# A fourth pair tile and a 512-token block with quarter products, in a retention layer followed by a gated feed-forward

## The chip, the cores and the metric

One core of a Trainium2 chip runs the kernel. The metric is the device time in microseconds. Three runs of the kernel before took 306.05, 307.16 and 307.43 us, so the median is 307.16.

## The reference

```python
# q, k, v: 8 batches x 8 heads x 576 positions x 64, float32
scores = scale * np.matmul(q, k.transpose(0, 1, 3, 2))
Dmat = np.where(rel >= 0, gamma[:, None, None] ** rel[None, :, :], 0.0)
attn_out = np.matmul(scores * Dmat[None, :, :, :], v)
x = attn_out.transpose(0, 2, 1, 3).reshape(4608, 512)
gate = 1.0 / (1.0 + np.exp(-(x @ w_gate)))    # 512 x 1536
val = x @ w_val                               # 512 x 1536
out = gate * val @ w_out                      # 1536 x 512
```

The decay by position is folded into two tables, by which q and k are multiplied when they are cast to bf16. What is left of the mask is a triangle of ones.

## The kernel before

The instructions stand in an order that the code writes out; no scheduler moves them. Engines are PE (TensorE), ACT (ScalarE), DVE (VectorE), POOL (GpSimd) and SP, which issues nearly all DMAs. Each engine works through its own queue in order and waits on semaphores.

**Attention.** A batch has 576 positions: four chunks of 128 and a last one of 64, which is put together with that of another batch. Attention within a chunk, or half a chunk, is a masked score product; what lies ahead comes in through a running state per head (k transposed times v). Two forms of this work exist.

- A *pair tile* takes 256 positions of one batch at once (`load_pair`, `cast_pair`, `pair_t`, `pair_qk`, `pair_st`, `third_intra`, `third_inter`, `pair_out`). Its q and k are transposed by PE. Before, there are three: batch 0 and batch 1, positions 0 to 255, and batch 0, positions 256 to 511.
- A *single chunk* or step takes 128 positions (`load_part`, `cast_qk`, `cast_v`, `cross` or `turn_step`, `scores`, `products`, `mask`, `intra`, `inter`). The transposed q and k (T) come by a DMA transpose on SP's queue (`cross`), or from PE for the steps in TURNED (0, 1 and 7). There are 30 steps before. Their matmuls are 64 wide and run in bursts: `slot_of_two` gives in one burst the values of up to two steps and the scores of up to two later ones. EARLY sets the bursts of the first blocks: the number of the place in the block, the steps whose values come, the steps whose scores come.

**Feed-forward.** Tokens go in blocks: 0 to 511, then 512 to 767, 768 to 1023, and from 1024 on blocks of 512. The first three blocks use plain matmuls, 256 columns wide in the blocks 512 and 768 (`h_units`, L817), then output products of 512 columns (`op_units`, L1157). Blocks from 1024 on use quarter products: of each unit of four 128-wide columns of w_gate or w_val, seven products of quarter size with sums of weights and of x take the place of eight. `quarter(kind, u, i)` is one of these, four matmuls of 256 columns (L941); g05 is gate unit 0, product 5, and w14 value unit 1, product 4. A unit has three PSUM banks, called a, g and e and listed in BANKS: the letters f, q, t, p, s are the bank pools. Product 1 goes to a, ACT copies a to g, product 2 is added there; 5 and then 3 go to e; 6, 7 and 4 are added in a. DVE adds what has to be summed, and ACT (gate) or DVE and POOL (value) take the results to SBUF. ORDER is the written order of these products in a block; in it a letter c is a part of a chunk's cast, x1d a sum of x on DVE, o a part of the output product.

The sums of weights are made once: `w_sums` for w_gate and w_val, `wo_sums` for w_out, all on DVE, at places given by SUMS_AT and PLACES in the blocks 512 and 768. The sums of x for a block (`x_sum`) are made on DVE or POOL when its attention is done.

**Queues around the change.** POOL multiplies k and q by the tables and casts v, chunk after chunk. SP issues a chunk's loads, then its transpose behind the loads of the next chunk, so loads stand behind a transpose that waits for POOL. `landing` deals the loads over 18 buffers.

**No-ops.** `space` puts a no-op behind a matmul of PE; SPACES and SPACES_FIRST say how many and in which blocks.

## Time and profile before

| | us |
|---|---|
| median of three runs | 307.16 |
| profiled execution | 306.89 |
| its span, first to last instruction | 305.2 |
| PE busy | 296.5 |
| DVE, ACT, POOL busy | 240.1, 195.0, 208.4 |
| block 512 begins, block 1024 begins (PE) | 53.46, 91.08 |

The span is what lies between the first and the last instruction; the 1.7 us beside it belong to the execution's time but have no instruction. Times in the views count from the span's start. A row of the chain or of a timeline has start, length, engine and what was done; "x8" are eight instructions merged, so that length/8 is the issue time of one.

### The profile page before, as it was taken

How to read it: one execution, taken by the hardware profiler on the slowest of the kernel's cores; microseconds unless marked ns; L12 is line 12 of the kernel's file. 1: busy time of each engine (PE TensorE's matmuls, PEld its weight loads, DVE VectorE, ACT ScalarE, POOL GpSimd, SP SyncE). 2: the span in 40 equal slices, each digit the busy share in tenths (PEclk: the TensorE clock that was granted, in tenths of full speed). 3: DMA queues.
4: the chain of work that ended last, by engine and by line, in shares of the span. 5: the costliest groups of instructions: out<-in, count | busy, mean ns of one | idle time of the engine just before them, and what ended most of it. 6: DMA issues, size and time to landing. Idle time of an engine off the chain costs nothing.

```text
span 305.2 us, 11063 instructions
## 1 busy us (share of the span) xinstructions
PE 296.5 (97%) x4473; PEld 242.7 (80%) x4483; DVE 240.1 (79%) x464; ACT 195.0 (64%) x414; POOL 208.4 (68%) x256
## 2 busy tenths in 40 slices
PE   7899999999999999999999999999999999999994
PEld 6754455876858888888888888888888888888883
DVE  4746786888897899689978997898789968945793
ACT  6534753426539656965796579657965886648640
POOL 5784543746466999769976997699769916741670
PEclk9999999999999999999999999999999999999998
DMA  7999998998999998999599939992960390022004
GB/s 216 317 350 397 358 272 200 211 211 175 188 174 228 188 249 198 237 250 217 134 197 238 198 70 216 231 191 66 229 159 4 102 248 3 2 61 81 2 2 138
DMA packets 145731, 54.99 MB, mean 180 GB/s; under 512 B 124048, under 2 KB 138640, under 8 KB 145680
## 3 DMA queue, kind: packets, MB, share of 16 engines
q1 hardware_dynamic: 144880, 53.63, 74.1%
q8 instruction: 36, 0.59, 0.8%
q10 hardware_dynamic: 800, 0.66, 0.7%
q14 instruction: 15, 0.12, 0.1%
HBM read 37.75 MB, written 9.44 MB: 155 GB/s over the span
## 4 chain that ended last, share of the span: by engine, by line
PE 93%; ACT 2%; DVE 1%; issue 1%; POOL 0%; ACTq 0%; POOLq 0%
PE gatea L941 12%; PE wa L941 12%; PE qa L1055 11%; PE qe L1055 9%; PE gatee L941 6%; PE we L941 6%; PE h_v L817 4%; PE h_g L817 3%; PE op L1157 3%; PE op L1431 3%; PE gateg L941 3%; PE wg L941 3%; PE val L656 2%; PE hv L1281 2%; PE hg L1281 2%; PE row L630 2%
## 5 line engine op out<-in xcount | busy, mean ns | idle before, releaser
L428 POOL TENSOR_TENSOR qk<-k,ktab 128x512 bf16<-128x512 f32 x30 | 32.3, 1078 | 7.0 <-DMA k<-in_k_dram 6.5
L1055 PEld LDWEIGHTS <-gsum 128*128 128x128 bf16 x336 | 31.9, 98 | 4.9 <-DVE gsum L878 0.8
L878 POOL TENSOR_TENSOR gsum<-gv 128x256 bf16<-128x256 bf16 (+1 forms) x35 | 26.8, 774 | 11.6 <-DVE gv L966 10.4
L941 PEld LDWEIGHTS <-wg_sb 128*128 128x128 bf16 x308 | 30.1, 98 | 3.7
L941 PEld LDWEIGHTS <-wv_sb 128*128 128x128 bf16 x308 | 30.1, 98 | 3.5
L428 POOL TENSOR_TENSOR qk<-q,qtab 128x512 bf16<-128x512 f32 x28 | 30.0, 1073 | 4.2 <-DMA q<-in_q_dram 4.2
L941 PEld LDWEIGHTS <-wvt 128*128 128x128 bf16 x280 | 27.4, 98 | 3.3
L941 PEld LDWEIGHTS <-wgt_sb 128*128 128x128 bf16 x252 | 24.6, 98 | 2.9
L1055 PEld LDWEIGHTS <-gv 128*128 128x128 bf16 x240 | 22.9, 98 | 3.1
L878 POOL TENSOR_TENSOR gsum<-gv,gsum 128x256 bf16<-128x256 bf16 x37 | 25.3, 715 | 0.0
L966 POOL TENSOR_TENSOR gv<-gv,wu 128x512 bf16<-128x512 bf16 x7 | 8.1, 1162 | 24.4 <-DVE wu L992 24.4
L645 DVE TENSOR_TENSOR pt<-row,tri 128x256 bf16<-128x256 f32 x60 | 21.2, 412 | 4.4 <-PE row L638 3.9
L433 POOL CAST v<-v 128x512 bf16<-128x512 f32 x20 | 13.7, 686 | 15.1 <-DMA v<-in_v_dram 11.0
L716 ACT CAST xT<-val 128x256 bf16<-128x256 f32 x60 | 18.9, 389 | 6.7 <-PE val L671 6.6
L941 PE MATMUL wa<-xsum,wv_sb 128*128 128x256 bf16 x140 | 21.0, 273 | 0.0
L607 ACT CAST sb<-s 128x256 bf16<-128x256 f32 x46 | 17.8, 418 | 4.6 <-DVE s L743 2.3
L941 PE MATMUL gatea<-xsum,wg_sb 128*128 128x256 bf16 x140 | 19.9, 273 | 0.0
L966 POOL TENSOR_TENSOR gv<-gv,ws 128x512 bf16<-128x512 bf16 x15 | 17.5, 1164 | 2.9 <-DVE ws L995 2.9
L995 DVE TENSOR_TENSOR gs<-gatea,gs 128x512 f32<-128x512 f32 x21 | 13.9, 688 | 6.0 <-PE gatea L941 5.2
L987 DVE TENSOR_TENSOR gatee<-gatea,gs 128x512 f32<-128x512 f32 x14 | 9.8, 699 | 10.2 <-PE gatea L941 7.4
L995 DVE TENSOR_TENSOR ws<-wa,ws 128x512 f32<-128x512 f32 x21 | 14.4, 685 | 4.2 <-PE wa L941 4.1
L964 ACT ACTIVATE gv<-gs 128x512 bf16<-128x512 f32 x21 | 13.0, 630 | 7.0 <-DVE gs L995 7.0
(191 smaller groups left out, 856.0 us busy)
## 6 DMA issues: line engine op xcount, KB each, us to landing
k<-in_k_dram SPq DMA_DIRECT2D x26, 256.0 KB, 4.7
q<-in_q_dram SPq DMA_DIRECT2D x26, 256.0 KB, 4.7
v<-in_v_dram SPq DMA_DIRECT2D x26, 256.0 KB, 4.3
out_dram<-ob SPq DMA_DIRECT2D x25, 256.0 KB, 3.5
wg<-in_moe_w_gate_dram SPq DMA_DIRECT2D x12, 256.0 KB, 5.3
wv<-in_moe_w_val_dram SPq DMA_DIRECT2D x12, 256.0 KB, 5.3
wo<-in_moe_w_out_dram SPq DMA_DIRECT2D x12, 256.0 KB, 5.0
v32p<-in_v_dram SPq DMA_DIRECT2D x6, 256.0 KB, 5.0
```

What stands on the lines that cost most here:

```text
L428: eng.tensor_tensor(out=natural_qk[s][:, i].rearrange("p m (y d) -> p y m d", y=2), in0=by_halves(loaded[s][1 - i]), in1=tab, op=ALU.mult)
L433: eng(out=natural["v", s], in_=loaded[s][2])
L607: eng(out=state[key], in_=src)
L645: nc.vector.tensor_tensor(out=probs[s][:, y], in0=row_ps[s][y][:, 0], in1=tri.unsqueeze(1).to_broadcast([P, M, 64]), op=ALU.mult)
L716: nc.scalar.copy(out=x_out(ALL, cols_of(s, i)), in_=x_in(val_ps[s][i], cols_of(s, i)))
L817: nc.tensor.matmul(ps[:, i], lhsT=w_sb[:, kc, (fc + i) * P:(fc + i + 1) * P], rhs=xT(kc, slice(t0, t0 + n)), start=(kc == 0), stop=(kc == ...
L878: eng.tensor_tensor(out=to, in0=a, in1=b, op=op)
L941: nc.tensor.matmul(ps[:, f], lhsT=w[:, kc, f * P:(f + 1) * P], rhs=x[:, kc], start=(first and f == 0 and kc == 0), stop=(f == 1 and kc == ...
L964: nc.scalar.activation(out=to, in_=src, func=AF.Sigmoid)
L966: eng.tensor_tensor(out=to, in0=to, in1=src, op=ALU.mult)
L995: nc.vector.tensor_tensor(out=me["s5"], in0=a, in1=me["s5"], op=ALU.add)
L1055: nc.tensor.matmul(ps[:, b], lhsT=left(fp)[:, b * P:(b + 1) * P], rhs=right(fp), start=(first and fp == 0 and b == 0), stop=(fp == NFC // ...
```

## The change

- A fourth pair tile, batch 1, positions 256 to 511, takes the place of the two single chunks (1, 2) and (1, 3). Its q, k and v are loaded in the places of the two chunks' loads, its transposes and scores stand between output products of the first block, and its values in block 512. 28 single steps are left; none of them is turned by PE.
- Tokens 512 to 1023 are one block. Units 0 and 1 of gate and value go by quarter products, unit 2 (`h_part`) by plain matmuls on half blocks. The order is ORDER_FIRST, with banks of its own (BANKS_FIRST). In it h80 is the gate product of columns 8 and 9 for the first 256 tokens, v81 the value product for the second 256, I and J are the values of the fourth pair and their way out, K and k a weight sum on POOL or DVE, C1 the casts of chunks up to 1, p a third of an output tile.
- The third weight sums of units 0 and 1 come earlier. The sums of unit 2 lie in block 512, five of the eight on POOL, and the twelve of w_out in block 1024 (SUMS_AT).
- Block 512 has three bursts of single steps where the two blocks had five.
- No-ops lie in other places: 40 and not 144 in the first block, 112 in block 1024, 60 in block 1536.

```diff
-    PAIRS = [(0, 0), (1, 0), (0, 1)]
+    PAIRS = [(0, 0), (1, 0), (0, 1), (1, 1)]
-    STEPS = [(1, 2), (1, 3)]
+    STEPS = []
...
-    SPACES = {2560: 40, 3072: 40}
-    SPACES_FIRST = 144
+    SPACES = {1024: 1, 1536: 1, 2560: 4, 3072: 4}
+    SPACES_OF = {1024: 112, 1536: 60, 2560: 40, 3072: 40}
+    SPACES_FIRST = 40
...
-    BLOCKS = [(512, 256), (768, 256)] + [(t, 512) for t in range(1024, NT, 512)]
+    BLOCKS = [(t, 512) for t in range(512, NT, 512)]
...
-    TURNED = (0, 1, 7)
-    def turn_step(s):
...
-            cast_qk(x, 0, nc.vector if x < 2 else nc.gpsimd)
-            if x not in TURNED:
-                cross(x)
+            cast_qk(x, 0, nc.gpsimd)
+            cross(x)
...
-    PLACES = (((1, 1), "g", 0), ((1, 2), "w", 0), ((2, 1), "w", 1), ((2, 2), "g", 1))
-    TURN_AT = ((1, (0, 3)), (7, (1, 11)))
...
+    BANKS_FIRST = {"g0": "f0 f1 t", "g1": "q0 f1 q1", "w0": "p f2 t", "w1": "s f1 q1"}
+    JOINED_FIRST = "g0 g1 w0 w1".split()
+    ORDER_FIRST = ("h80 v80 I h90 J v90 g01 X1d w01 X2d C0 g02 X3p g05 X4d w02 g11 g06 g15 K g12 g16 C1 g03 w05 g07 g13 g17 w06 w11 g04 C2 w15 w03 g14 K "
+                   "w12 w07 w16 h81 w04 C3 v81 w13 w17 h91 w14 v91 K p p C4 p K p C5 p p K p p p k p k p k p").split()
...
+    def h_part(gvs, t0, what, fc, x):
+        gv_tile(gvs, t0, fc)
+        cols = slice(x * 256, (x + 1) * 256)
+        to = made[t0, fc // 4][:, fc % 4:fc % 4 + 2, cols]
+        at = (1, 2)[what == "v"] if x == 0 else (0, 2)[what == "v"]
+        ps = ffn_psum.tile([P, 2, 256], FP32, tag="ffn", name=f"h_{what}_{t0}_{fc}_{x}", at=at)
+        for i in range(2):
+            for kc in range(NKC):
+                nc.tensor.matmul(ps[:, i], ...)
+        if what == "h":
+            nc.scalar.activation(out=to, in_=ps, func=AF.Sigmoid)
+        else:
+            nc.vector.tensor_tensor(out=to, in0=to, in1=ps, op=ALU.mult)
...
+    store(opps[1], P, on_act)
+    turn("k", 3, 0, *TR)
+    cast_pair("v", 3, 0, on_pool)
+    cast_pair("v", 3, 1, on_pool)
+    store(opps[2], 2 * P, on_dve)
+    opps.append(ffn_psum.tile([P, 512], FP32, tag="ffn", name="op_0_3", at=0))
+    op_first(range(0, 2), (3,), opps)
+    turn("q", 3, 0, *PV)
+    op_first(range(2, 4), (3,), opps)
+    turn("k", 3, 1, *QK[0])
+    op_first(range(4, 6), (3,), opps)
+    turn("q", 3, 1, *QK[0])
+    op_first(range(6, 8), (3,), opps)
+    pair_qk(3, 0, [TR, PV])
+    op_first(range(8, 10), (3,), opps)
+    pair_qk(3, 1, QK)
+    op_first(range(10, NFC), (3,), opps)
+    pair_st(3, ST, TR)
...
+    def last_pair():
+        third_intra(3, [PV, QK[0]])
+        third_inter(3, True)
+        mark(*ST)
+    def last_pair_out():
+        mark(*ST)
+        third_inter(3, False)
+        pair_out(3, 0, on_act)
+        pair_out(3, 1, on_act)
...
-    SUMS_AT = {0: (0, 1, 2, 3, 4, 5, 11, 12, 13, 15, 16, 17), 1: (0, 1, 3, 4, 5, 7, 9, 11)}
-    EARLY = (((6, [], [0, 1]), (13, [0, 1], [2, 3])), ((2, [2, 3], [4]), (7, [4], [5]), (13, [5], [6, 7])))
+    SUMS_AT = {1: tuple(range(0, 40, 3))}
+    EARLY = (((36, [], [0, 1]), (40, [0, 1], [2, 3]), (45, [2, 3], [4, 5])),)
```

What this does to the queues is seen best at three places. In these rows a name's number is a buffer, and the semaphores that an instruction waits for stand in brackets.

On PE, in block 512, the end of g03 (written to gatee, bank t) and the beginning of w05 (written to we, bank t too), new in this block:

```order
L934 MATMUL gatee_0_1428<-xT_1118,wgt_sb 128x256 [waits DVE_49]
L934 LDWEIGHTS wgt_sb
L934 MATMUL gatee_0_1428<-xT_1118,wgt_sb 128x256
L934 LDWEIGHTS wvt_827
L934 MATMUL we_0_1500<-xsum_0_1285,wvt_827 128x256 [waits Activation_49]
L934 MATMUL we_0_1500<-xsum_0_1285,wvt_827 128x256
```

w05 follows g03 at once, and its first matmul waits for ACT.

On ACT, where block 1024 begins, before (ob is an output tile's copy, xT a chunk's values on their way to x, gateg the first copy of block 1024):

```order
L849 COPY ob_2303<-op_0_2159 128x512 [waits PE_49]
L716 CAST xT_1950<-val_0_2169 128x8x32
L716 CAST xT_1950<-val_1_2170 128x8x32
L607 CAST sb_0_0_2328<-s_3_0_0_2314 128x256 [waits DVE_49]
L607 CAST sb_0_1_2330<-s_3_0_1_2316 128x256 [waits DVE_49,Activation_49]
L849 COPY ob_2336<-op_1_2308 128x512 [waits PE_49,Pool_49]
L976 COPY gateg_0_2345<-gatea_0_2340 128x512 [waits PE_49,Activation_49]
```

and now:

```order
L843 COPY ob_1981<-op_2_1956 128x512 [waits PE_49,Pool_49]
L711 CAST xT_1948<-val_0_1990 128x8x32 [waits PE_49]
L711 CAST xT_1948<-val_0_1990 128x8x32
L843 COPY ob_2164<-op_3_1985 128x512 [waits DMAHW4_49,PE_49]
L711 CAST xT_1948<-val_1_1991 128x8x32 x2
L602 CAST sb_0_0_2179<-s_3_0_0_2169 128x256 [waits DVE_49]
L602 CAST sb_0_1_2181<-s_3_0_1_2171 128x256 [waits DVE_49]
L969 COPY gateg_0_2193<-gatea_0_2184 128x512 [waits PE_49,Activation_49]
```

The copy of the block's last output tile stood behind all casts to x and now stands ahead of the last two.

On DVE, at the beginning of block 1024, before:

```order
L899 TENSOR_TENSOR xsum_1_2323<-xT_1950,xsum_0_2322 128x512
L368 TENSOR_TENSOR wv_sb<-wv_sb 128x2x256
L368 TENSOR_TENSOR wg_sb<-wg_sb 128x2x256
L987 TENSOR_TENSOR gatee_1_2356<-gatea_1_2348,gs_1024_1_2361 128x512
L987 TENSOR_TENSOR gatee_0_2400<-gatea_0_2340,gs_1024_0_2405 128x512
L995 TENSOR_TENSOR gs_1024_1_2361<-gatea_1_2348,gs_1024_1_2361 128x512
```

and now:

```order
L893 TENSOR_TENSOR xsum_1_2174<-xT_1948,xsum_0_2173 128x512
L329 TENSOR_TENSOR wt_sb<-wo_sb 128x512
L329 TENSOR_TENSOR wt_sb<-wo_sb,wt_sb 128x512
L980 TENSOR_TENSOR gatee_1_2208<-gatea_1_2197,gs_1024_1_2217 128x512
L329 TENSOR_TENSOR apart_830<-wo_sb 128x512
L980 TENSOR_TENSOR gatee_0_2273<-gatea_0_2184,gs_1024_0_2282 128x512
L329 TENSOR_TENSOR wt_sb<-wo_sb,wt_sb 128x512
L988 TENSOR_TENSOR gs_1024_1_2217<-gatea_1_2197,gs_1024_1_2217 128x512
```

Between the sums that gate products wait for there now stand the sums of w_out (wt_sb and apart from wo_sb), twelve in all.

More of the change, by code (lines that the diff above doesn't have):

```diff
@@ L215 @@
     load_w(8, 4)
-    pair_2 = load_pair(2)
-    for n_wo, n_pair in ((6, 4), (2, 2), (4, 0)):
+    later = [one for A in (2, 3) for one in [load_pair(A)] * 6]
+    for n_wo, n_pair in ((6, 4), (2, 2), (4, 6)):
         for _ in range(n_wo):
@@ L220 @@
         for _ in range(n_pair):
-            next(pair_2)
+            next(later.pop(0))
     LEAD_CAST = 3
@@ L383, in dealt @@
     def dealt(cols):
-        return max(b for b in [(0, 0)] + BLOCKS if b[0] <= cols.start)[1] == 512
+        return cols.start >= BLOCKS[1][0]
     def x_out(rows_, cols):
@@ L547, in third_inter @@
                     kc = 2 * y + u
[L548 to L550 removed]
+                    nc.tensor.matmul(pair_ps[2 * A + a][kc][0][half(x), kc, :],
+                                     lhsT=state[PAIRS[A][0], 1 + a, 1][half(y), 2 * u + x, :],
+                                     rhs=turned["qp", A][half(y), 2 * u + x, a * P:(a + 1) * P],
                                      start=False, stop=(u == 1), skip_group_check=True)
@@ L910, in bank @@
         def bank(kind, u, i):
-            which = BANKS[kind + str(u)].split()[i]
-            if t0 == BLOCKS[2][0] and kind + str(u) == "g0" and i == 1:
-                which = FIRST_G
+            which = (BANKS if t0 > BLOCKS[0][0] else BANKS_FIRST)[kind + str(u)].split()[i]
             pool, tag = FROM_POOL[which[0]]
@@ L982, in quarter @@
                 me["both"] = me.get("both", 0) + 1
-                if kind + str(u) not in JOINED:
+                if kind + str(u) not in joined:
                     if i == 6:
@@ new lines @@
+    running[1] = new_state((1, 2, 1), FP32)
+    nc.vector.tensor_tensor(out=running[1], in0=first[:, 1], in1=st_tiles[3, 0], op=ALU.add)
+    keep_state((1, 2, 1), running[1], on_act)
+    state[1, LAST - 1, NJ - 1] = new_state((1, LAST - 1, NJ - 1))
+    nc.vector.tensor_tensor(out=state[1, LAST - 1, NJ - 1], in0=running[1], in1=st_tiles[3, 1], op=ALU.add)
+    for kind in "gw":
+        w_sums(kind, 2, 1, nc.vector)
+    loads_to(6)
+    def last_pair():
+        third_intra(3, [PV, QK[0]])
+        third_inter(3, True)
+        mark(*ST)
```

143 lines of the change are left out of this document (75 added, 68 removed).

## The prediction

> **What bounds the kernel now.** First the page's busy shares and the chain of waits, to see which engine sets the end.
>
> ```profile
> PE 296.5 (97%) x4473; PEld 242.7 (80%) x4483; DVE 240.1 (79%) x464; ACT 195.0 (64%) x414; POOL 208.4 (68%) x256
> PE 93%; ACT 2%; DVE 1%; issue 1%; POOL 0%; ACTq 0%; POOLq 0%
> ```
>
> The tensor engine (PE) is 93% of the chain that ended last. A busy PE need not be a full one, so the list of what PE waited for comes next, and busy time by stage: the 512-token blocks 512 and 768 are split at 71.9, then the gate and value products of block 1024.
>
> ```profile
> PE op L1157 <- issue: 0.3, 2, 0.2
> PE row L638 <- issue: 0.3, 1, 0.3
> ...
> PE op L1431 <- issue: 0.2, 1, 0.2
> ```
>
> ```profile
> 53.40:71.90 18.50, 18.29 (x322) 13.97 (x322) 16.02 (x34) 8.32 (x19) 10.86 (x12) 1.00 1.04 205
> 71.90:91.10 19.20, 18.99 (x371) 14.44 (x372) 16.07 (x37) 9.49 (x24) 10.31 (x11) 1.00 0.96 183
> 91.10:110.20 19.10, 19.10 (x177) 17.10 (x176) 15.30 (x26) 14.63 (x27) 15.24 (x17) 1.00 1.06 214
> ```
>
> (Columns after the length: PE, weight loads, DVE, ACT, POOL, then clock, DMA share, GB/s.) From 53 to 110 us PE never stands for more than a few tenths, at full clock. So two rules follow: a matmul that is taken away is worth its whole issue time, and any new wait of PE is paid whole, because there is no slack into which it could fall. The chain of waits gives the issue times:
>
> ```profile
> 39.14 1.44 PE op L1431 x6
> ...
> 51.73 1.73 PE op L1431 x8
> 53.46 0.87 PE h_g L817 x8
> ...
> 56.95 0.45 PE turn L592 x8
> ...
> 59.15 0.87 PE h_g L817 x8
> 60.69 0.98 PE h_v L817 x8
> ...
> 91.08 0.87 PE gatea L941 x8
> ...
> 110.07 0.65 PE qa L1055 x6
> 112.05 1.42 PE qe L1055 x12
> ...
> 114.78 1.31 PE qe L1055 x12
> 117.22 1.42 PE qa L1055 x12
> ```
>
> A 256-column matmul takes 0.87/8 = 0.109 us, a 512-column one 1.73/8 = 0.216, a turned step 0.45.
>
> **The change, first the PE work.** It all lies between 39.14 and 91.08. What follows is the same in kind: 22 single chunks are left to the later blocks in both kernels.
>
> 1. Gate and value products of tokens 512 to 1023: 192 matmuls of 256 columns before; now 28 quarter products of 4 and 8 half-block groups of 8, that is 176. 16 x 0.109 = -1.75.
> 2. Three turned steps go (two are the chunks that the pair replaces, the third now goes by DMA transpose): 3 x 0.45 = -1.35.
> 3. Five attention bursts become three. The five before: from 53.46 to 91.08 are 37.62 us, less 192 x 0.109 = 20.93, less two turns 0.90, less 48 x 0.216 = 10.38, leaves 5.41. The three now, each by its nearest of the same make-up: scores alone 0.78 (59.15 + 0.87 to 60.69 + 0.11, since the group behind takes 0.98 for 0.87); two chunks' values with two chunks' scores 1.44 (110.72 to 112.05 + 0.11); values with one and a half scores 1.24 (116.09 to 117.22 + 0.11). Sum 3.46: -1.95.
> 4. The fourth pair comes in, with the instructions of the third. From 39.14 to 53.46 are 14.32, less 48 x 0.216 and one turn: 3.49. Its scores now stand in two groups, a further switch between large and small matmuls of 0.1 to 0.2: +3.6.
>
> Sum -1.4 (bounds -1.9 and -0.9, since a burst of the same make-up differs by some 0.2). The removed work is small because the pair's work takes back most of it.
>
> **The waits that it adds.** In the new order several products stand right behind the instruction that frees what they need. Three latencies carry these:
>
> ```profile
> 54.17 1.04 PE L817 MATMUL h_v<-xT,wv_sb 128*128 128x256 bf16 x8
> ```
>
> ```profile
> 54.37 0.60 ACT L820 ACTIVATE gv<-h_g 128x512 bf16<-128x512 f32 x1 [0.23 <-PE h_g L817]
> ...
> 69.42 0.59 ACT L849 COPY ob<-op 128x512 f32<-128x512 f32 x1 [4.46 <-PE op L1157]
> 69.90 1.21 ACT L716 CAST xT<-val 128x256 bf16<-128x256 f32 x4
> ...
> 89.00 0.66 ACT L716 CAST xT<-val 128x256 bf16<-128x256 f32 x2
> ...
> 91.65 1.08 ACT L976 COPY gateg<-gatea 128x512 f32<-128x512 f32 x2
> ```
>
> ```profile
> 6.12 0.70 ACT qT L465
> 6.86 0.69 PE qkp L474 x16
> ```
>
> PE passes on from a gate group to the next group at 54.17 and ACT begins on the group left at 54.37: 0.20. The sigmoid takes 0.60. From ACT's end (6.82) to a waiting PE (6.86): 0.04.
>
> 5. g03 and w05 both write bank t, and w05 stands right behind g03. So w05 waits for the sigmoid that empties g03: 0.20 + 0.60 + 0.04 = +0.84. Everything behind it on PE waits too. In block 1024 the same two products have different banks (f1 and t).
> 6. g02 writes the bank into which ACT copies g01, with only w01 between: 0.20 + 0.54 (two copies take 1.08) + 0.04 less the 0.44 of w01 = +0.34. ACT comes from casting pair 3 just then and is not earlier.
> 7. Block 1024's first product, g01, reads the even columns of all its 512, so the last cast of chunks 2 and 3 too. On ACT this cast stands behind the copy of the last output tile of block 512, which waits for that tile's last matmul, and that is the last PE work of the block. PE waits 0.20, then the copy until the next may begin (69.42 to 69.90, 0.48), the two casts (0.66), 0.04: +1.38. Before, these casts were over at 89.66, 1.4 ahead of 91.08. DVE, which frees that product's bank by the state sums, ends about then, so it adds nothing.
> 8. w14 needs the DVE sum of w17's result. Between the sum that frees w04 and this one DVE has five other results.
>
> ```profile
> 96.79 1.29 DVE L995 TENSOR_TENSOR gs<-gatea,gs 128x512 f32<-128x512 f32 x2 [0.87 <-PE gatea L941]
> ```
>
> One takes 0.69, the next begins 0.60 after it: six are 3.7. PE has w04, v81, w13, w17 and h91 in that time, 3.06, and comes to w04 some 0.3 after it was freed. About 0.35 late, with 0 and 0.7 as bounds: +0.35.
>
> **Sums of w_out.** Twelve of these DVE sums leave the blocks 512 and 768 and now lie between the gate results of block 1024.
>
> ```profile
> 70.03 1.12 DVE L328 TENSOR_TENSOR wt_sb<-wo_sb,wt_sb 128x512 bf16<-128x512 bf16 x1
> ...
> 72.18 0.42 DVE L328 TENSOR_TENSOR wt_sb<-wo_sb,wt_sb 128x512 bf16<-128x512 bf16 x1
> 72.52 0.42 DVE L328 TENSOR_TENSOR wt_sb<-wo_sb 128x512 bf16<-128x512 bf16 x1
> ...
> 89.69 1.44 DVE L899 TENSOR_TENSOR xsum<-xT 128x512 bf16<-128x512 bf16 x2
> ...
> 91.84 1.28 DVE L368 TENSOR_TENSOR wv_sb<-wv_sb 128x512 bf16<-128x512 bf16 x1
> 93.04 0.41 DVE L368 TENSOR_TENSOR wg_sb<-wg_sb 128x512 bf16<-128x512 bf16 x1
> ...
> 106.14 0.69 DVE L995 TENSOR_TENSOR gs<-gatea,gs 128x512 f32<-128x512 f32 x1
> ```
>
> ```profile
> 69.82 1.04 POOL L428 TENSOR_TENSOR qk<-q,qtab 128x512 bf16<-128x512 f32 x1
> ```
>
> ```profile
> 107.07 0.60 PE L941 MATMUL gatea<-xsum,wg_sb 128*128 128x256 bf16 x4
> ```
>
> 9. In 91.1 to 110.2 DVE is busy 15.30 of 19.10: 3.8 free. Two weight sums leave (1.28 + 0.41), two sums of x that lay ahead of the stage come in (1.4): 4.1 free. The tightest place is g24 at 107.07, whose sum ends at 106.83, a margin of 0.24. Alone, a sum takes 0.34 to the next (72.18 to 72.52): 12 x 0.34 = 4.1, no wait. Beside a POOL multiplication it took 1.12 (70.03, with POOL's from 69.82 to 70.86). I take 0.43, three quarters alone and a few long ones as it was before: 12 x 0.43 = 5.2, less 4.1 and 0.24, about +0.9. The upper bound is the second rival.
>
> **Transposes.** POOL has x sum 3 (X3) ahead of chunk 1's casts. It waits for pair 3's last cast, so the casts that feed DMA transposes start late.
>
> ```profile
> 56.60 1.35 SPq L437 DMA_TRANSPOSE T<-qk  x1
> ...
> 77.58 2.91 SPq L437 DMA_TRANSPOSE T<-qk  x1
> ```
>
> 10. Four rounds of loads and a transpose took 21.0 here, and SP holds later loads behind each transpose. After pair 3's casts (about 60.6), X3, a weight sum and chunk 1's two casts, transpose 1 goes at about 65; four such rounds end at 86, and landing 3 to 4 later meets the third burst, which stands near 89. Bounds 0 and 2, taken +0.3. Pair 3's loads themselves are as many and as large as those of the two chunks they replace.
>
> What costs nothing: the no-ops on PE and the weight sums given to POOL.
>
> ```profile
> L253 PEldq NOP  x224: 13/13/13, 17.3 to 228.9; - x112
> ```
>
> Block 1024 gets 112 of these, 1.5 us on the weight-load side, which is busy 17.10 of 19.10 in its gate stage: it stays under the matmuls. POOL's weight sums are hidden as long as the transposes are; if not, each adds about a POOL multiplication (1.04) to point 10.
>
> **Sum.** -1.4 + 0.84 + 0.34 + 1.38 + 0.35 + 0.9 + 0.3 = +2.7. The profiled execution took 306.89 us (span 305.2), so 309.6; the median of the runs, 307.16, lies 0.27 above it: **309.9 us**, slower by 0.9%.
>
> **Rivals.**
>
> R1, not slower: the waits 8 to 10 stay away, since each wait of PE lets DVE and POOL catch up, and PE work falls by its lower bound. It decides at g24: if DVE runs ahead of PE there, only the three waits for ACT are left, 2.56 - 1.9 = +0.7, or 307.8. If in addition the 0.8 us that the list of waits puts down to "issue", which stands beside the bursts, goes with two of the bursts: 307.0. For it: DVE's idle time in the stage is as large as the sums alone. Against it: POOL is busy 15.24 of 19.10 there. To be faster by 0.5% it would have to lose two of the waits 5 to 7 as well, which the order of the instructions does not allow; a quarter of R1 stands for a price there that I have read wrong.
>
> R2, DVE becomes the bound of block 1024. POOL is busy in 0.8 of that stage; with six sums at 0.55 and, where POOL has least idle time, six at 0.8, both between the 0.34 and the 1.12, they take 8.1, 4.0 more than is free; less 0.24, PE waits 3.8 and not 0.9: 312.8. For it: the 1.12 beside POOL and the 1.28 at 91.84. Against it: at 72 DVE ran alone, and a waiting PE also thins POOL's work. [...]
>
> R3, the transpose of chunk 5 lands 2 us behind the burst: 311.6. For it: in the kernel before the order avoids it by turning step 7 on PE. Against it: DMA has some us free while POOL waits.
>
> **Chances.** Forecast 0.47, R1 0.23, R2 0.22, R3 0.08. What a measurement of this kernel can tell from no change is about 0.5%, 1.5 us: 305.6 to 308.7. Of R1 a quarter would be faster, the rest the same; of the forecast a small part falls under 308.7: faster 0.06, same 0.23, slower 0.71. Range 307.0 to 312.8: the low end takes in most of R1, the upper one R2.
>
> **What would show it.** In the changed profile: PE waits for ACT of about 0.8 at the first w_e product of block 512 and of 1.4 at block 1024's first gatea; one near 0.35 at g02. The rows of the w_out sums between 93 and 110 give R2 or R1: means near 0.4 or near 0.9, with or without PE waiting for DVE at gatea. A PE wait for a DMA transpose in the last burst of block 512 is R3. Block 1024 beginning later than 91.1 by 1.5 to 2.2 us confirms points 1 to 8. I am wrong if block 1024 begins at 91 or earlier.

## The result, and the profile after

The changed kernel takes 315.34 us (median of 314.92, 315.15, 315.53 and 317.53), the kernel before in the same measurement 306.61 us (305.16 to 307.43). The ratio is 1.0305, with a 95% interval from 1.024 to 1.0369: slower by 8.7 us, where 309.9 us with a range from 307.0 to 312.8 was forecast. The direction is the one forecast, the size is three times as large. The profiled execution took 315.53 us, its span is 313.8, 8.6 more than before.

First the busy shares and the chain of waits, from the page of the changed kernel.

```profile
PE 296.4 (94%) x4428; PEld 240.1 (77%) x4439; DVE 246.6 (79%) x463; ACT 199.4 (64%) x419; POOL 218.1 (69%) x264
PE 74%; DVE 9%; DMA 7%; issue 2%; ACT 2%; POOL 2%; SPq 2%; POOLq 0%; DVEq 0%
```

PE is busy as long as before, but only 74% of the chain is PE's now, where it was 93%. DVE is busy 6.5 us longer than before, POOL 9.7; time in which an instruction is held up counts as busy (of the sums of w_out shown below, the one at 101.22 is a single row of 1.28 us, the one at 99.04 of 0.43).

Where the time lies is seen from PE's timeline: the first product of block 1024 and of block 1536, before and after. (This view gives 90.91 for block 1024, the chain in the prediction 91.08. The differences below all come from the timeline.)

```profile
90.91 0.82 PE L941 MATMUL gatea<-xT,wg_sb 128*128 128x256 bf16 x6
...
121.20 0.60 PE L941 MATMUL gatea<-xT,wg_sb 128*128 128x256 bf16 x4
```

And after; here with all the places from the first block's output products to block 1024 at which PE waited 0.17 us or more for another engine (in brackets its idle time and what ended it):

```profile
51.39 0.59 PE L1467 MATMUL op<-wo_sb,gv 128*128 128x512 bf16 x2 [0.93 <-DVE ob L843]
...
62.03 0.60 PE L934 MATMUL gateg<-xT,wg_sb 128*128 128x256 bf16 x4 [0.28 <-ACT gateg L969]
62.80 0.60 PE L934 MATMUL gatee<-xsum,wgt_sb 128*128 128x256 bf16 x4 [0.17 <-DVE xsum L893]
...
66.48 0.60 PE L934 MATMUL gatee<-xT,wgt_sb 128*128 128x256 bf16 x4 [0.47 <-DVE gatee L980]
67.76 0.60 PE L934 MATMUL we<-xsum,wvt 128*128 128x256 bf16 x4 [0.69 <-ACT gv L957]
...
78.11 0.60 PE L934 MATMUL wa<-xsum,wv_sb 128*128 128x256 bf16 x4 [0.48 <-DVE ws L988]
...
91.84 0.32 PE L625 MATMUL row<-T 64*64 64x64 bf16 x16 [0.80 <-DMA T<-qk]
...
95.47 1.03 PE L934 MATMUL gatea<-xT,wg_sb 128*128 128x256 bf16 x8 [1.22 <-ACT xT L711]
...
129.88 0.60 PE L934 MATMUL gatea<-xT,wg_sb 128*128 128x256 bf16 x4
```

Each bracket is some 0.16 less than what the place costs, since the row of the matmul ahead still runs in that time (a row of four is 0.60 long, and where nothing is waited for the next begins 0.44 behind its start, as at 67.76 and 68.20). Measured from start to start, less the matmul's own 0.109 (0.216, 0.054), the eight places cost 1.09, 0.44, 0.34, 0.63, 0.85, 0.64, 0.99 and 1.39, together 6.4 us. From the first product of a stage to the first of the next:

| us | before | after |
|---|---|---|
| first block's output products to block 512 | 14.32 | 17.23 |
| block 512 to block 1024 | 37.61 | 39.45 |
| block 1024 | 30.29 | 34.41 |
| block 1536 to PE's last product | 179.76 | 179.78 |

So half of the loss lies ahead of block 1024 and half in it; from block 1536 on nothing changed. How full DVE is in the two middle stages, by windows (length, then PE, weight loads, DVE, ACT, POOL, clock, DMA share, GB/s), before:

```profile
53.30:90.90 37.60, 37.18 (x689) 28.33 (x692) 31.98 (x69) 17.81 (x42) 21.27 (x23) 1.00 1.00 195
90.90:121.20 30.30, 30.30 (x490) 26.84 (x488) 25.78 (x50) 21.34 (x46) 26.00 (x31) 1.00 1.01 214
```

and after:

```profile
95.40:129.80 34.40, 31.19 (x488) 26.55 (x488) 33.59 (x61) 21.63 (x48) 27.82 (x32) 1.00 0.92 185
```

In block 1024 DVE is busy 33.59 of 34.40 us, 7.8 more than before. PE now waits for it there, which it did nowhere in this block before. From the list of PE's waits in the whole changed kernel (us in total, times, longest):

```profile
PE wa L934 <- DVE ws L988: 1.1, 2, 0.6
...
PE gatee L934 <- DVE gv L959: 0.9, 1, 0.9
...
PE we L934 <- DVE wu L985: 0.7, 1, 0.7
...
PE wa L934 <- DVE we L980: 0.5, 1, 0.5
...
PE gatea L934 <- DVE gs L988: 0.2, 1, 0.2
```

One of the two waits in the first row is that of w14 in block 512. The other five, with a small one at 100.12, cost 4.12 us from start to start, which is the whole loss of the block. The twelve sums alone are more than DVE's 7.8: their rows add up to 9.55, a mean of 0.80; less 0.08, by which a row overlaps the next, 0.72 each where 0.43 was forecast. The groups of these sums in the changed kernel (busy, mean ns of one) and some of them beside POOL's instructions, in order of time:

```profile
L329 DVE TENSOR_TENSOR wt_sb<-wo_sb,wt_sb 128x512 bf16<-128x512 bf16 x6 | 5.0, 838 | 0.0
L329 DVE TENSOR_TENSOR wt_sb<-wo_sb 128x512 bf16<-128x512 bf16 x3 | 2.7, 899 | 0.0
L329 DVE TENSOR_TENSOR apart<-wo_sb 128x512 bf16<-128x512 bf16 x3 | 1.8, 606 | 0.0
```

```profile
61.32 1.15 POOL L893 TENSOR_TENSOR xsum<-xT 128x512 bf16<-128x512 bf16 x1 [6.52 <-ACT xT L590]
61.59 1.16 DVE L893 TENSOR_TENSOR xsum<-xT 128x512 bf16<-128x512 bf16 x1
...
99.04 0.43 DVE L329 TENSOR_TENSOR wt_sb<-wo_sb,wt_sb 128x512 bf16<-128x512 bf16 x1
...
101.18 1.04 POOL L430 TENSOR_TENSOR qk<-k,ktab 128x512 bf16<-128x512 f32 x1 [0.76 <-PE wa L934]
101.22 1.28 DVE L329 TENSOR_TENSOR wt_sb<-wo_sb,wt_sb 128x512 bf16<-128x512 bf16 x1
...
104.52 1.04 POOL L430 TENSOR_TENSOR qk<-k,ktab 128x512 bf16<-128x512 f32 x1 [0.37 <-DMA k<-in_k_dram]
104.80 1.04 DVE L329 TENSOR_TENSOR wt_sb<-wo_sb,wt_sb 128x512 bf16<-128x512 bf16 x1
```

The reader is to add start and length. POOL's instructions end at 62.47, 102.22 and 105.56; the sums that began beside them end at 62.75, 102.50 and 105.84, each 0.28 later, whenever they began. The sum at 99.04 has no POOL instruction beside it as it begins and takes 0.43. Of the twelve sums ten begin while a POOL instruction runs, and each of the ten ends 0.28 after that instruction; an eleventh begins in the last 0.01 us of one and takes 0.41. So each of these ten, a DVE sum of two SBUF operands, was held until POOL's instruction was over, and 0.28 longer. DVE's operations that take one operand from a PSUM bank were not: the one at 102.42 (gs<-gatea,gs) begins beside POOL's multiplication from 102.18 to 103.40 and takes 0.68, and the one at 113.70 (gv<-gv,wa), with POOL idle, 0.68 as well.

### The profile page after: what moved, and what is told of

Its sections match the earlier page's. It is cut to its first block, busy times and chain, and to the rows that moved or that the text cites. A ratio compares the mean times of both kernels' runs of the same rounds, so it can differ in the third digit from the quotient of the medians.

```text
span 313.8 us, 11063 instructions
## 1 busy us (share of the span) xinstructions
PE 296.4 (94%) x4428; PEld 240.1 (77%) x4439; DVE 246.6 (79%) x463; ACT 199.4 (64%) x419; POOL 218.1 (69%) x264
## 4 chain that ended last, share of the span: by engine, by line
PE 74%; DVE 9%; DMA 7%; issue 2%; ACT 2%; POOL 2%; SPq 2%; POOLq 0%; DVEq 0%
PE qa L1049 11%; PE gatea L934 11%; PE wa L934 11%; PE qe L1049 9%; PE we L934 6%; PE gatee L934 6%; PE wg L934 3%; PE gateg L934 2%; DMA v<-in_v_dram 2%; PE hv L1318 2%; PE hg L1318 2%; DVE gv L959 2%; DMA T<-qk 2%; DMA v32p<-in_v_dram 1%; PE val L651 1%
## 5 line engine op out<-in xcount | busy, mean ns | idle before, releaser
L934 PEld LDWEIGHTS <-wg_sb 128*128 128x128 bf16 x340 | 33.2, 98 | 6.3 <-PE op L1151 1.4
L934 PEld LDWEIGHTS <-wv_sb 128*128 128x128 bf16 x340 | 33.2, 98 | 5.9 <-issue 2.2
L934 PEld LDWEIGHTS <-wvt 128*128 128x128 bf16 x304 | 29.7, 98 | 5.4 <-issue 1.9
L430 POOL TENSOR_TENSOR qk<-k,ktab 128x512 bf16<-128x512 f32 x28 | 30.7, 1095 | 4.2 <-DMA k<-in_k_dram 3.4
L934 PEld LDWEIGHTS <-wgt_sb 128*128 128x128 bf16 x276 | 27.0, 98 | 5.5 <-issue 2.5
L934 PE MATMUL wa<-xsum,wv_sb 128*128 128x256 bf16 x156 | 23.4, 272 | 1.6 <-DVE ws L988 1.1
L640 DVE TENSOR_TENSOR pt<-row,tri 128x256 bf16<-128x256 f32 x56 | 19.9, 414 | 6.3 <-PE row L633 5.0
L934 PE MATMUL gatea<-xsum,wg_sb 128*128 128x256 bf16 x156 | 22.2, 273 | 0.2 <-DVE gs L988 0.2
L988 DVE TENSOR_TENSOR gs<-gatea,gs 128x512 f32<-128x512 f32 x23 | 15.3, 687 | 7.1 <-PE gatea L934 6.3
L435 POOL CAST v<-v 128x512 bf16<-128x512 f32 x19 | 12.8, 672 | 8.4 <-DMA v<-in_v_dram 8.2
L988 DVE TENSOR_TENSOR ws<-wa,ws 128x512 f32<-128x512 f32 x23 | 15.8, 685 | 3.5 <-PE wa L934 3.5
```

The costliest lines, as they stand in the source:

```text
L430: eng.tensor_tensor(out=natural_qk[s][:, i].rearrange("p m (y d) -> p y m d", y=2), in0=by_halves(loaded[s][1 - i]), in1=tab, op=ALU.mult)
L435: eng(out=natural["v", s], in_=loaded[s][2])
L640: nc.vector.tensor_tensor(out=probs[s][:, y], in0=row_ps[s][y][:, 0], in1=tri.unsqueeze(1).to_broadcast([P, M, 64]), op=ALU.mult)
L934: nc.tensor.matmul(ps[:, f], lhsT=w[:, kc, f * P:(f + 1) * P], rhs=x[:, kc], start=(first and f == 0 and kc == 0), stop=(f == 1 and kc == ...
L988: nc.vector.tensor_tensor(out=me["s5"], in0=a, in1=me["s5"], op=ALU.add)
```

## The experiments

The stages of all runs, from PE's timeline of each profile, and the total of w_out's sums in block 1024 (their rows' lengths added). The ratios given with the runs are to the kernel before in the same measurement.

| run | first block's output | block 512 | block 1024 | sums in 1024 |
|---|---|---|---|---|
| before | 14.32 | 37.61 | 30.29 | none |
| after | 17.23 | 39.45 | 34.41 | 12, 9.55 |
| e1, sums early | 17.03 | 40.07 | 32.52 | none |
| e2, POOL reads nothing | 17.02 | 39.89 | 32.01 | 12, 6.46 |
| e3, X3 on DVE | 17.36 | 37.84 | 33.98 | 12, 8.69 |
| e7, before with late sums | 14.65 | 37.42 | 32.55 | 12, 7.18 |
| e4, four orders | 16.43 | 38.52 | 34.46 | 12, 9.05 |
| e5, all edits | 18.22 | 40.00 | 32.57 | none |
| e6, plain block 512 | 17.03 | 39.89 | 32.92 | 12, 6.91 |
| e8, POOL ahead | 16.77 | 40.27 | 34.65 | none |
| e9, the same, sums in 1024 | 17.49 | 37.40 | 33.62 | 12, 8.53 |
| e10, the same, no sums | 17.91 | 37.36 | 30.24 | none |

The theory is that DVE's sums, held up by POOL, made block 1024 and the beginning of block 512 long. The rival is that there are simply too many of them, or that the block begins late for another reason.

**e1: the sums elsewhere.**

```diff
     store(opps[2], 2 * P, on_dve)
+    wo_left = [... the twelve wo_sums ...]
+    for _ in range(4):
+        wo_left.pop(0)(nc.vector)
...
-    SUMS_AT = {1: tuple(range(0, 40, 3))}
+    SUMS_AT = {0: (1, 1, 1, 1, 1, 41, 42, 44)}
```

> The changed kernel with one edit: the twelve DVE sums of w_out leave block 1024; four stand behind the copy of the third output tile, five behind the first value product of block 512 (where DVE and, in the changed kernel's trace, POOL too stood idle from 59 to 61 us), three between the output products of block 512. In the changed kernel block 1024 takes 34.4 us from its first product to the next block's, 4.1 more than before. If the sums in that stage are the cause (second rival of the prediction): 30.3 to 30.8, and the whole 3.4 to 4.1 less, 311.2 to 311.9 us, less up to 1 us that the sums may cost where they now stand. If instead the stage is slow because its x sums start with it and not ahead of it: the stage stays at 33 or more and the time at 314 or more.

Measured: 312.82 us, ratio to before 1.0201 (1.0176 to 1.0225). The gate and value products of block 1024, up to its first output product, fall from 22.11 to 17.96 us; 17.90 it was before. So the sums are all of the loss in these products. But the whole block takes 32.52, since its output products now wait, as the list of PE's waits shows:

```profile
PE qa L1049 <- POOL gsum L872: 1.2, 1, 1.2
...
PE qa L1049 <- DVE gsum L872: 0.5, 1, 0.5
```

These are sums of gate times value, made by POOL. POOL's first multiplication of the block by a value product starts here and in the kernel before at:

```profile
107.98 1.61 POOL L959 TENSOR_TENSOR gv<-gv,wu 128x512 bf16<-128x512 bf16 x1
```

```profile
101.09 1.16 POOL L966 TENSOR_TENSOR gv<-gv,wu 128x512 bf16<-128x512 bf16 x1
```

That is 12.8 us behind the block's first product (95.19), and 10.2 before (90.91). POOL is 2.6 us later in line: the change has it one chunk's casts behind, and these casts wait for loads (the last one 1.48 us for k). In the changed kernel this is hidden, because the slow gate stage gives POOL the time.

**e2: POOL's multiplications read nothing.** For steps 6 to 9, whose casts fall into block 1024, POOL fills q and k with a constant.

```diff
+        if 6 <= s <= 9:
+            eng.memset(natural_qk[s][:, i], 0.01)
+            return
```

> The changed kernel, but POOL fills the k and q of steps 6 to 9 with a constant in place of multiplying them by the tables, so that these instructions read nothing (the output of these chunks is not the reference's). The twelve sums stay on DVE in block 1024. Theory 1, DVE's sums are held up by POOL's instructions: their mean falls from 0.80 us to 0.5 or less, block 1024 from 34.4 us to 31.5 or less, the time to 312.5 or less. Theory 2, twelve sums are too many for DVE in that stage whatever POOL does: the stage stays at 33.5 or more, the time at 314.4 or more.

Measured, in a single run: block 1024 32.01 us, 2.4 less; the sums' mean 0.54; the time 312.67. That is most of the way to theory 1, though none of its three bounds (31.5, 0.5, 312.5) is quite reached. A fill also takes only half as long as a multiplication (two take 0.98, one multiplication 1.04), so POOL has less to do as well; what holds the sums up is told by the rows:

```profile
100.44 0.98 POOL L430 MEMSET qk<- 128x512 bf16 x2
100.60 0.41 DVE L329 TENSOR_TENSOR wt_sb<-wo_sb,wt_sb 128x512 bf16<-128x512 bf16 x1
...
103.32 0.99 POOL L430 MEMSET qk<- 128x512 bf16 x2
103.69 0.41 DVE L329 TENSOR_TENSOR wt_sb<-wo_sb,wt_sb 128x512 bf16<-128x512 bf16 x1
...
105.39 1.35 POOL L962 TENSOR_TENSOR gv<-gv,ws 128x512 bf16<-128x512 bf16 x1
...
106.24 0.78 DVE L329 TENSOR_TENSOR wt_sb<-wo_sb,wt_sb 128x512 bf16<-128x512 bf16 x1
```

Beside a fill a sum takes its 0.41; beside POOL's product of gate and value, which reads SBUF and was left as it was, the sum at 106.24 ends at 107.02, again 0.28 behind POOL's 106.74. So in this run being beside POOL cost nothing by itself; being beside a POOL instruction that reads did. All six sums up to 104, two of them beside a fill, took 0.41 or 0.42; of the six behind, five began beside such an instruction and took 0.50 to 0.99.

**e3: the third sum of x on DVE.**

```diff
-    ... C0 g02 X3p g05 X4d ...
+    ... C0 g02 X3d g05 X4d ...
```

> The changed kernel with one letter changed: the third sum of x of block 512 on DVE and no longer on POOL. POOL then isn't held for 6.5 us by pair 3's last cast; its weight sum and chunk 1's casts run ahead of the x sums. Theory 1 (POOL's instructions hold DVE's sums): the waits of 0.34 at g05 and 0.63 at g03 in block 512 go, and the transpose that came 0.99 late for the third burst is in time: 1.9 less, 313.4 us. Theory 2 (DVE only has too many sums there): one more on DVE leaves the wait at g05, adds 0.34 at g03, and only the transpose is in time: 0.6 less, 314.7 us.

Measured: 313.53 us, ratio 1.0229 (1.02 to 1.0258), 1.9 less in the span, the size of theory 1. With one sum more on DVE, the waits for DVE at g05 and g03 are gone: with POOL's sum gone and its weight sum and casts run ahead, only one of the sums of x meets POOL, and four take 2.4 us (61.55 to 63.94) where three took 3.6. The transposes come sooner too, but the third burst still waits, 0.56 and not 0.99; block 1024 is 0.43 shorter, which happens to make up for that.

**e7: the late sums alone, in the kernel before.**

```diff
-    SUMS_AT = {0: (0, 1, 2, 3, 4, 5, 11, 12, 13, 15, 16, 17), 1: (0, 1, 3, 4, 5, 7, 9, 11)}
+    SUMS_AT = {0: (0, 1, 2, 3, 4, 5, 11, 12), 1: (), 2: tuple(range(0, 40, 3))}
```

> The kernel before with one part of the change alone: its twelve sums of w_out stand on DVE in block 1024, not in the blocks 512 and 768. If these sums among POOL's instructions are what makes that block slow: its 30.3 us become 33.3 to 34.4 and the time 309.6 to 311 us. If the slow block needs the rest of the change too (a late last cast and x sums that begin with the stage): at most 0.9 more, as the forecast had it, 307.5 us or less.

Measured: 309.70 us, ratio 1.0095 (1.0063 to 1.0128), some 3 us more. Block 1024 takes 32.55 us, 2.3 more: less than the 3 to 4.1 expected, more than the forecast's 0.9. (Another 0.7 lies ahead of block 512, where the edit changes nothing.) Here POOL is a chunk further, six of the twelve sums begin with no POOL instruction beside them or in the last 0.01 us of one, and the mean is 0.60. So the price is not a constant of the sums; it depends on where POOL stands.

**e4: four places put in another order.**

```diff
-    op_first((11,), range(3), opps)
-    store(opps[0], 0, on_dve)
+    op_first((11,), (2, 0, 1), opps)
+    store(opps[2], 2 * P, on_dve)
+    store(opps[0], 0, on_dve)
...
-    ... g03 w05 g07 g13 g17 w06 ... h91 w14 v91 ...
+    ... g03 g07 g13 w05 g17 w06 ... h91 v91 w14 ...
...
             (in op_units, the last output tile)
-            store(opp, t0 + nb * P)
-            yield 4 * 512
+            yield 4 * 512
+        store(opp, t0 + nb * P)
```

> The changed kernel with four changes of order and nothing else: the last products of the first block's third output tile and its copy come first, since the fourth tile takes that bank; w05 stands two products later; w14 behind v91; the copy of block 512's last output tile behind the last casts to x. In the changed kernel these places cost 1.09, 0.85, 0.64 and 1.39 us. Theory A, each wait stands for itself: they fall to about 0.4, 0, 0 and 0.1, 3.4 less, 312.0 us. Theory B, the transpose of chunk 5 lands when POOL and SP's queue let it, whatever PE does: PE reaches the third burst 2.0 us earlier, waits 3.0 and not 0.99 there, and only the last place brings something: 1.3 less, 314.1 us.

Measured: 314.94 us, ratio 1.0265 (1.0196 to 1.0334); the span 1.3 shorter. Of the waits at op_0_3, w05 and w14, 2.58 together, 0.29 is left at the first. But two waits stand in PE's list in their place:

```profile
PE row L625 <- DMA T<-qk: 1.2, 1, 1.2
PE gatea L934 <- DVE s L738: 1.1, 1, 1.1
```

The transpose costs 1.40 and not 0.99, and at the beginning of block 1024 PE waits 1.30 for DVE's state sums where it waited 1.39 for ACT's casts: taking the copy out of ACT's way won 0.1. Neither theory held: the transpose takes back a fifth of what the other places give, not all of it, and the last place, the only one that counts in theory B, brings next to nothing. That the span falls by theory B's 1.3 is chance.

**e5: all edits together,** e1, e3 and e4.

> The changed kernel with the edits of the three earlier ones together: w_out's sums ahead of block 1024, the third sum of x on DVE, and the four changes of order. If the causes are those named and independent, what is left of the change is its PE work and the 0.44 at g02: 306.4 - 1.6 + 0.4 + 0.4 = 305.6 us, just faster than the kernel before. If the late transpose and, behind it, POOL's late sums in the output stage of block 1024 (2.0 us of waits in the run with the early sums) take the place of the waits: 307.5 to 309.5 us.

Measured: 316.53 us, ratio 1.0308 (1.0247 to 1.0368), no better than the change itself; both expectations are missed. From PE's list in the profiled execution (314.89):

```profile
PE gatee L934 <- DVE xsum L893: 1.6, 1, 1.6
PE qe L1049 <- ACT ob L1094: 1.3, 1, 1.3
PE h_v L1176 <- DVE gv L1182: 1.1, 1, 1.1
...
PE st L506 <- DVE ptp L489: 0.8, 1, 0.8
```

With the third sum of x gone from POOL, POOL casts chunks and makes two weight sums between 51 and 68 us, just where e1 had put nine of the sums. Six of the nine are held up there, and the masks and products behind them in DVE's queue with them. By these rows the edits do not add up because each moves the meeting of DVE and POOL to another place. Of the 2.3 that block 1024 is longer than before, 1.48 is the wait for ACT's copy of an output tile (the second row), whose cause is open, and 0.85 one for a late sum on POOL.

**e6: block 512 with plain products.**

```diff
-    ORDER_FIRST = ("h80 v80 I h90 J v90 g01 X1d w01 ... h91 w14 v91 K p p C4 ...")
+    ORDER_FIRST = ("h80 v80 I h90 J v90 C0 h00 v00 h20 v20 K C1 h40 v40 ... h61 v61 K p p C4 ...")
...
-    EARLY = (((36, [], [0, 1]), (40, [0, 1], [2, 3]), (45, [2, 3], [4, 5])),)
+    EARLY = (((24, [], [0, 1]), (28, [0, 1], [2, 3]), (33, [2, 3], [4, 5])),)
```

The bursts stay where they were; their places have other numbers because the block has twelve products fewer ahead of them.

The third sums of w_gate and w_val stand by then where raw weights of units 0 and 1 stood, so the output of this block is not the reference's; the instructions and their times are those of plain products.

> The changed kernel with one part undone: all gate and value products of block 512 are plain products on half blocks, 192 matmuls of 256 columns as in the kernel before and not 176; no sums of x there. The fourth pair, the three bursts and the sums in block 1024 stay. Theory 1, quarter products there cost more in waits than they save: 1.75 more PE work, less the waits at g02, g05, g03, w05 and w14 (2.9) and some 0.4 of the late transpose: 1.6 less, 313.8 us. Theory 2, the waits only change their place, since DVE and ACT have as much to do: 315.3 to 317 us.

Measured: 314.09 us, ratio 1.0215 (1.0154 to 1.0276). The size is that of theory 1, the way is another: block 512 is 0.4 longer than with quarter products, not shorter, and block 1024 is 1.5 shorter, since POOL is further and the sums take 6.91 and not 9.55. In block 512 the five waits go (2.9), and so do those for the transpose and for ACT's casts (2.4); 1.75 of matmuls and a wait of 2.5 us for DVE's state sums at its end come, and 1.4 more from the edit itself. All value products here use one bank, and ten of the groups wait 0.14 us for DVE to empty it:

```profile
62.50 0.69 DVE L1180 TENSOR_TENSOR gv<-gv,h_v 128x512 bf16<-128x512 bf16 x1 [1.20 <-PE h_v L1174]
...
63.24 1.03 PE L1174 MATMUL h_v<-xT,wv_sb 128*128 128x256 bf16 x8
```

DVE ends at 63.19 and PE begins 0.05 behind. In the kernel before, plain products have no such wait. So the quarter products there save nothing net: with plain ones as they were before, block 512 would by this estimate be 1 us shorter than with quarter ones.

**e8, e9, e10: POOL ahead.** All three have e3's edit, e4's orders, chunk 4's casts ahead of POOL's part in w11 (behind which POOL stood for 12.8 us in e5, as the next row, POOL's timeline there, shows), and the third burst one place earlier. e8 has the twelve sums between the output products of block 512, e9 in block 1024, e10 leaves them out.

```profile
81.19 1.16 POOL L959 TENSOR_TENSOR gv<-gv,ws 128x512 bf16<-128x512 bf16 x1 [12.78 <-DVE ws L988]
```

```diff
-    ... w04 C3 v81 w13 w17 h91 w14 v91 K p p C4 p K p C5 ...
+    ... w04 C3 C4 v81 w13 w17 h91 v91 w14 K p p p K p C5 ...
...
-    EARLY = (((36, [], [0, 1]), (40, [0, 1], [2, 3]), (45, [2, 3], [4, 5])),)
+    EARLY = (((36, [], [0, 1]), (40, [0, 1], [2, 3]), (44, [2, 3], [4, 5])),)
(e8 alone)
-    SUMS_AT = {1: tuple(range(0, 40, 3))}
+    SUMS_AT = {0: (37, 38, 38, 39, 39, 41, 42, 42, 43, 43, 44, 44)}
```

> The changed kernel with the orders of the earlier run (third output tile first, w05 two products later, w14 behind v91, last copy behind the casts), the third sum of x on DVE, POOL's casts of chunk 4 ahead of its part in w11 (behind which POOL stood for 12.8 us in the run with all edits), the third burst one place earlier, and the twelve sums of w_out between the output products of block 512, where the kernel before had such sums. Theory A, what made the changed kernel slow is DVE beside POOL and POOL's place in line, and both are now away: block 512 to block 1024 takes 36.6 to 37.5 us in place of 39.45, block 1024 30.3 to 31.3, the whole 306 to 308 us, level with the kernel before. Theory B, DVE and POOL together have too much to do in block 512, with sums of x, products in quarters and sums of weights in one block: the waits appear at other places there, or as POOL's late sums in block 1024's output stage, 309.5 us or more.

Measured: 314.14 us, ratio 1.0245 (1.0211 to 1.0278): theory B. Sums among POOL's casts and the bursts of attention hold up the masks and the state sums, and PE waits for these: 1.4 at the bursts, 2.5 at the beginning of block 1024. Its block 1024 is long for another reason, told under the last heading.

> The last kernel (POOL's casts ahead, the orders of block 512) with the twelve sums of w_out back where the change has them, in block 1024. Theory A, the price of the sums in block 1024 is their DVE time less the 4.1 us that DVE has free there, and with POOL one chunk ahead they take about 0.5 each: block 1024 takes 32.2 to 32.6 us, as in the kernel before with late sums, and not 34.4; block 512 without those sums no longer waits for DVE at its bursts and at its end and takes 36.5 to 37.5 from its first product to block 1024's; the whole 309 to 311 us. Theory B, block 512 is too full by itself, sums or not: it stays at 39 or more, the whole 312 us or more.

Measured: 312.62 us, ratio 1.0175 (1.0149 to 1.0201). Block 512 takes the expected 37.40, so it isn't too full by itself; block 1024 takes 33.62 and not 32.2 to 32.6, as the mean of the twelve was 0.71, not 0.5: the sums met POOL again, since alone one takes 0.41 to 0.43. So the whole stays above theory A's 309 to 311.

> The same, but the twelve sums of w_out are left out everywhere (the tiles are filled with a constant in the first block, so the outputs from token 1024 on are not the reference's). It gives what the change is worth where DVE has no place to put these sums. Theory A: block 1024 takes 30.3 us as before, the whole 306.5 to 308.5 us: even so not faster than the kernel before by more than a measurement can tell. If POOL or the x sums make block 1024 slow by themselves: 31.5 us or more there, the whole 309 us or more.

Measured: 316.69 us, ratio 1.0295 (1.0248 to 1.0342). This time is no measure of the change: DVE's fills hold up the first block, whose output products begin 4.0 us later than in e9. The profiled execution took 313.93, the other three 316.58 to 317.09. The stages behind the fills can be read in its profile: block 1024 takes 30.24 us, as before, with POOL's work and the sums of x in it. Taking 4.0 off the span of 312.2 gives 308.2, still 3.0 above the kernel before. The first block's output products are 3.6 longer than there, of which some 1.5 is a reduced clock in this run (last heading): their first ten matmuls, six large ones and four small, take 2.99 us from 42.85 to 45.84, and at the full clock's 0.216 a large one and 0.23 for four small ones (as at 47.51) they would take 1.53. In block 512 only 0.25 is won.

No version came below the kernel before.

## Why the prediction was right or wrong

The prediction's sum was +2.7; by the same points the profile gives +8.7:

| point | forecast | measured |
|---|---|---|
| 1 to 4, PE's work | -1.4 | -1.6 |
| 5, w05 behind g03 | +0.84 | +0.85 |
| 6, g02 | +0.34 | +0.44 |
| 7, last casts behind the copy | +1.38 | +1.39 |
| 8, w14 | +0.35 | +0.64 |
| 9, twelve sums in block 1024 | +0.9 | +4.12 |
| 10, transpose of chunk 5 | +0.3 | +0.99 |
| not listed: op_0_3 1.09, g05 0.34, g03 0.63 | 0 | +2.06 |

(The rows add up to 8.9; the first block's output begins 0.2 earlier in the profile after.)

**PE's work** was right: 16 matmuls of 0.109 fewer are 1.75, and what is left of the two stages when these matmuls, the 96 large ones and the waits are taken off is 10.39 us against 10.26, where 0.3 more was forecast.

**The three waits for ACT** (5 to 7) were right to 0.1, each worked out from one latency, one duration and what lies between. The clause that DVE adds nothing at the beginning of block 1024, as it "ends about then", held as well, but e4 shows the other side of it: with ACT out of the way DVE is the next, 0.1 behind.

**Point 9 is the step that failed,** and in it one factor. Its account was right: DVE's time for the twelve sums, less what is free, is what PE waits. By the table of runs, the total of the sums' rows against what block 1024 takes above 30.29: 9.55 and 4.1, 9.05 and 4.2, 8.69 and 3.7, 8.53 and 3.3, 7.18 and 2.3, 6.91 and 2.6, 6.46 and 1.7, none and 0 (e10; e1, e5 and e8 have none there either and are longer for other reasons, told above and under the last heading). The difference stays between 4.3 and 5.4; less twelve overlaps of 0.08, 3.3 to 4.5 us are free, and the prediction had 4.1 and 0.24. What was mis-sized is one sum: 0.43, "three quarters alone and a few long ones", where it was 0.72. The prediction had quoted the row that shows the price (the sum at 70.03, which ends 0.29 behind POOL's instruction) and POOL's share of the stage (15.24 of 19.10), and then did not put the two together. Put together afterwards they give this estimate. A sum that begins anywhere in the stage meets POOL 8 times in 10, waits for half of an instruction of some 1.0 us and needs 0.28 more: 0.8 x 0.78 + 0.2 x 0.41 = 0.71, less the overlap 0.63. Twelve are 7.6, less 4.1 and 0.24 makes +3.2. Measured were ten meetings in twelve and +4.12. That is the second rival, with its 3.8; it was given 0.22 because at one place, 72 us, DVE had run alone, and because a waiting PE would thin POOL's work. The range ended at 312.8, where this rival alone leads; what lies above it is about the unlisted waits, 0.7 of the transpose and 0.3 of w14.

**The unlisted waits,** 2.06 us that the prediction had at nothing, have two causes. g05 and g03 wait because three DVE sums of x stand beside three POOL instructions in a row (61.59 to 65.2, where alone they would take 1.1); point 10 speaks of POOL's third sum only as delaying POOL. It is the same factor as in point 9, and e3 removes both. op_0_3 is a mistake of reading: the fourth output tile goes into the bank of the third one, whose copy is the second of two in DVE's queue; the change adds a reader of the order of copies that the prediction did not follow. e4 takes 0.8 of its 1.09 away.

**Points 8 and 10** had the right mechanism and lay within their bounds, 0 to 0.7 and 0 to 2. e3 and e4 show that the transpose is a second bound right behind: it gives back part of what is won ahead of it.

**What would show it:** the waits of 0.8 at the first w_e product and 1.4 at block 1024, the small one at g02 and the long sums with PE waiting for DVE are as described. Block 1024 beginning 1.5 to 2.2 later was not: it began 4.6 later.

What stays open: e1's and e5's late sums of gate times value are put down to POOL's place in line by their rows alone, and e5's late copy on ACT has no cause named; e8 and e9, with POOL a chunk ahead, don't have these waits, but differ in more than that.

## What to carry to other kernels

Before moving DVE sums like these (128x512, bf16, both operands in SBUF) into a stage, take POOL's busy share there as a first estimate of the chance that each is held until POOL's current instruction is over, and price it with half of POOL's instruction and 0.28 us, not with its duration alone. Here the share was 0.8, and in the profiles after and e7 ten and six of the twelve were held, so bounds are needed beside the estimate. DVE, busy 15.30 of the stage's 19.10 us, had room for fewer sums than the forecast's price said: its 3.8 us of idle time hold almost nine at 0.43 and five at the 0.72 that they took. A saving of 1.6 us on the busiest engine was paid for with 6.5 us of DVE and 9.7 of POOL that had no free place. And a freed wait should be followed to the next engine in line: here ACT, DVE and the transpose stood within 0.1 to 1 us of each other, so removing one of them won little.

## What the runs showed of the hardware that was not expected

**0.28 us behind POOL.** In three profiles (after, e2, e7) 21 of w_out's 36 sums in block 1024 begin beside a POOL instruction that reads SBUF, a cast, a multiplication or a sum; all 21 end 0.28 us behind its end, to 0.01. The other 15 take 0.41 to 0.43: two beside a constant fill, three that begin in the last 0.01 us of a POOL instruction, and ten with no POOL instruction beside them as they begin. In five of these ten one begins while the sum runs, and the sum pays nothing.

**A waiting PE lost its clock in two runs.** In e8, windows over the beginning of block 1024 (PE, weight loads, DVE, ACT, POOL, then the granted clock) and PE's timeline:

```profile
96.00:100.00 4.00, 2.88 (x17) 1.72 (x15) 3.96 (x5) 2.35 (x5) 3.80 (x5) 0.65 1.01 224
100.00:104.00 4.00, 4.00 (x21) 2.82 (x19) 1.57 (x3) 1.37 (x3) 0.49 (x1) 0.50 0.97 217
104.00:108.00 4.00, 4.00 (x39) 3.58 (x38) 2.25 (x4) 3.44 (x7) 0.00 (x0) 1.00 1.04 230
```

```profile
95.63 1.03 PE L934 MATMUL gatea<-xT,wg_sb 128*128 128x256 bf16 x8 [2.52 <-DVE s L738]
97.72 1.01 PE L934 MATMUL gatee<-xsum,wgt_sb 128*128 128x256 bf16 x4 [1.05 <-DVE xsum L893]
98.52 1.06 PE L934 MATMUL wa<-xT,wv_sb 128*128 128x256 bf16 x4
...
103.89 0.65 PE L934 MATMUL we<-xsum,wvt 128*128 128x256 bf16 x4
```

After waits of 2.52 and 1.05 us with 0.9 of work between them, the clock granted is one half from 97.2 to 104.0, a matmul takes 0.213 and not 0.109, and 3.1 us are lost, nearly as much as by the waits themselves. With the 1.2 that the second wait costs, this is why e8's block 1024 took 34.65 in the profiled execution (316.08; the median is 314.14). In e10 the same follows two waits in the first block:

```profile
42.00:44.00 2.00, 2.00 (x7) 0.77 (x7) 1.91 (x4) 0.00 (x0) 1.12 (x3) 0.68 0.83 237
44.00:46.00 2.00, 2.00 (x9) 1.01 (x8) 1.97 (x4) 0.00 (x0) 1.53 (x2) 0.50 1.03 301
```

There PE had waited 1.06 ahead of 37.16 and 2.66 ahead of 41.94. A single wait of 2.29 in e6 left the clock at 1.00 (windows from 90 to 106), and so did all waits of the changed kernel (1.00 in its windows from 0 to 313).

By the means of the windows, one half lasts 6.8 us in e8 (97.2 to 104.0) and 3.4 in e10 (42.7 to 46.2). In e8 the fall lies within the second wait, 4.1 us behind the beginning of the first; in e10 it lies 0.8 behind the end of the second. PE was busy 1.48 of the 4.00 us from 92.00 to 96.00 in e8, 0.06 of the 2.00 from 40.00 to 42.00 in e10, and in e6, where the clock stayed, 0.31 of the 2.60 from 93.00 to 95.60. Three cases do not show what decides, the longest wait, the sum of the waits or PE's work beside them. Nor are such waits the only case: in e4, e5 and e7 the page's row of the clock has 0.7 in the second of its 40 slices (some 7.8 us each), where the kernel before and the changed one have 0.9 or more, and why is not shown.
